# Attention with two branches on one core: the keys' maximum rounded in one step, and three orders given to the planner

## The chip, the cores and the metric

The kernel runs on one core of a Trainium2 chip. The metric is the device time of one execution in microseconds. The program is ordered by hand-written planning code: five engines (TensorE or PE for matmuls, VectorE or DVE, ScalarE or ACT, GpSimd or POOL, and SP, which only issues transfers) each run their own list of instructions, and wait for each other through semaphores.

## What is computed

The input `x` has 2048 rows of 512. Branch A is full attention with 32 heads of 16 dimensions, branch B attends to 8 earlier rows at a distance of 2; the two results are mixed by a gate of each row.

```
g = sigmoid((x * gate_w).sum(-1))
A: q, k, v = x @ A_wqkv;  p = softmax(q k^T / 4) over all 2048 keys;  a = (p v) @ A_wo
B: q, k, v = x @ B_wqkv;  keys and values at s, s-2, ..., s-14;       b = (p v) @ B_wo
out = g * a + (1 - g) * b
```

## The kernel before

**Branch A.** The 2048 queries are cut into 4 chunks of 512 columns, the 32 heads into 8 groups of 4. A pair of (chunk, group) is a *period*: 32 of them, in this order. In a period each of the 4 heads meets 16 tiles of 128 keys; one such meeting is a *unit*: a score matmul of 128 keys x 512 queries, an exponential, and a matmul of the result with the values. Most units go to ScalarE, in *sets* of 3 and 2 units that alternate between two score buffers in PSUM (`rA`, `rB`, the tile `ring`): TensorE writes `ring` from `kt_all` (keys) and `qt` (queries), ScalarE writes `pT` by one ACTIVATE of 1536 or 1024 columns, TensorE multiplies `pT` with `vp_all` (values with a column of ones, for the denominator) into an accumulator. In every period some units (3 at first, 12 from the ninth on) go to VectorE instead, which approximates the exponential by integer arithmetic: `dt_a` or `wkv` from the scores, then three shifted copies `pd_a`, multiplied with scaled values `vd_all`.

Instead of the row's maximum, the scores get a bound: a query's 32 rows of `qt` hold it and its absolute values, the keys' rows hold the keys and, in the other half, minus the largest absolute key (`negk`). `k_proj` projects one group's keys for one chunk of rows, and its VectorE instruction also leaves the maximum over 512 columns in `kmax_all`. `k_bound` (L663) then takes the maximum of four such columns (`mx`), swaps rows with two matmuls against `perm` (`sw`, which wants 16-bit operands: `kmax_b`), makes `negk` of it (`ng`), and writes it into the keys (`fill`). For the first group this stands on the way to the first exponential.

**Other producers.** `v_proj` projects values; for the first group of heads it is called twice, for tiles 0 to 7 and 8 to 15, with 32 matmuls each. `q_proj` projects the queries of the first two periods; `q_pair` those of two later periods at once, which go through DRAM (`q_scr`) and come back by two transfers on SP. Branch B (`b_tile`) projects its keys and values (`bw`), sends them through DRAM (`kv_scr`, `ksh`, `vsh`) and works mostly on POOL.

**The order.** Every step is an `Op` with an engine, an expected length, a due time (`dl`), dependencies, buffers that it takes, and an earliest time (`rel`). `list_schedule` goes through them once as the program is built, with its own clock, takes on each engine the step that is due first among those that can start, and may put filler matmuls on zeros (`z`) between TensorE's steps so that it stays busy. Three PSUM banks (tile `misc_ps`) serve all projections, VectorE's scores and the accumulator. The result is one fixed list for each engine. So a changed due time, length or earliest time can change the lists everywhere behind it. `S0[p]` is the planned start of period p.

Of the kernel before, what the change touches and what calls it, by code (L numbers as in the profile page):

```python
# [9 lines left out]
ALU = mybir.AluOpType  # L10
AX = mybir.AxisListType
FP32 = mybir.dt.float32
# [16 lines left out]
NG = 8  # L29
# [73 lines left out]
QD = 20.0  # L103
# [198 lines left out]
def kernel(  # L302
# [26 lines left out]
    const = ctx.enter_context(tc.tile_pool(name="const", bufs=1))  # L329
# [37 lines left out]
    V = Chained(nc.vector, "dve")  # L367
# [22 lines left out]
    def op(eng, occ, fn, dl, **kw):  # L390
        if any(tk.kind == "misc" for tk in kw.get("use", ())):
            dl -= URG[eng]
        o = Op(eng, occ, fn, dl, **kw)
        ops.append(o)
        return o
# [61 lines left out]
    S0 = [T0 + UNIT * f for f in first_unit]  # L457
# [25 lines left out]
    vp_all = const.tile([128, NT, H, DH + 1], BF16, name="vp_all")  # L483
    vd_all = const.tile([128, NV - 1, NTD, H, DH + 1], BF16, name="vd_all")
    kmax_all = const.tile([128, NG, NC], FP32, name="kmax_all")
    kmax = const.tile([128, NG], FP32, name="kmax")
    kmax_b = const.tile([128, NG], BF16, name="kmax_b")
    negk = const.tile([128, NG], FP32, name="negk")
    dt_a = const.tile([128, NDE * NGR * QW], BF16, name="dt_a")
# [153 lines left out]
    o_kc = {}  # L643
# [20 lines left out]
    def k_bound(i, dl):  # L664
        st = {}
        tk = tok("acc", 1) if i == 0 else tok("misc", 2)

        def mx():
            V.tensor_reduce(out=kmax[:, i:i + 1], in_=kmax_all[:, i, :], axis=AX.X, op=ALU.max)
            V.tensor_copy(out=kmax_b[:, i:i + 1], in_=kmax[:, i:i + 1])  # L670

        def sw():
            st["p"] = misc_ps([128, 2], tag="acc" if i == 0 else "misc")
            for e in range(2):
                mm(st["p"][:, e:e + 1], perm[:, e].rearrange("p a b d -> p (a b d)"), kmax_b[:, i:i + 1], True, True)

        def ng():
            V.scalar_tensor_tensor(out=negk[:, i:i + 1], in0=st["p"][:, 0:1], scalar=st["p"][:, 1:2], in1=rowc[:, 2:3],
                                   op0=ALU.max, op1=ALU.mult)

        def fill(s0, s1):
            def s():
                V.tensor_scalar(out=kt_all[:, i, s0:s1], in0=kt_all[:, i, s0:s1], scalar1=rowc[:, 1:2],
                                scalar2=negk[:, i:i + 1], op0=ALU.mult, op1=ALU.add)
            return s
        a = op("dve", 0.4, mx, dl - 2.5, deps=o_kc[i])
        b = op("pe", 0.1, sw, dl - 2.0, full=0, deps=[a, o_perm], alloc=[tk])
        c = op("dve", 0.2, ng, dl - 1.2, deps=[b], use=[tk])
        if i == 0:
            o_k[i] = [op("dve", 0.0, fill(sc * QW, (sc + 1) * QW), dl + 0.1 * sc, deps=[c], parts=SB(QW)) for sc in range(NC)]  # L690
        else:
            o_k[i] = [op("dve", 0.0, fill(0, S), dl, deps=[c], parts=SB(S))] * NC
# [14 lines left out]
    def v_proj(h0, h1, tb, TB, tag, dl, rel=0.0):  # L707
        n = (h1 - h0) * DH
        st = {}
        tk = tok(tag, 2 if tag == "misc" else 1)  # L710

        def mk(half):
            def s():
                if half == 0:
                    st["pv"] = misc_ps([128, TB, n], tag=tag)
                for tt in range(half * TB // 2, (half + 1) * TB // 2):
                    t = tb + tt
                    for c in range(DC):
                        mm(st["pv"][:, tt, :], xT[:, c, t * 128:(t + 1) * 128],
                           wkv[:, c, D + h0 * DH:D + h1 * DH], c == 0, c == DC - 1)  # L720
            return s

        def ev():
            V.tensor_copy(out=vp_all[:, tb:tb + TB, h0:h1, 0:DH], in_=st["pv"][:].rearrange("p t (h d) -> p t h d", d=DH))

        t0 = max(tb, NT - NTD)
        nt = tb + TB - t0

        def evd():
            w = wts[:]  # L730
            k0, n_ = t0 - (NT - NTD), (h1 - h0) * (DH + 1)
            V.tensor_tensor(out=vd_all[:, :, k0:k0 + nt, h0:h1, :].rearrange("p m t h d -> p m t (h d)"),
                            in0=_ap(vp_all[:, t0, h0, 0:1], [list(vp_all[:].ap[0]), [0, NV - 1], [H * (DH + 1), nt], [1, n_]]),
                            in1=_ap(w, [list(w.ap[0]), [1, NV - 1], [0, nt], [0, n_]]), op=ALU.mult)
        xs = [o for sc in range(NC) if sc * TPC < tb + TB and (sc + 1) * TPC > tb for o in o_xt[sc]]
        a = op("pe", 0.62, mk(0), dl - 2.0, full=2, deps=[o_wv] + xs, alloc=[tk], rel=rel, name=f"vp{h0}.{tb}")
        b = op("pe", 0.62, mk(1), dl - 1.4, full=2, deps=[a], use=[tk])
        c = op("dve", 0.61, ev, dl, deps=[b, o_init_p], use=[tk])
        for h in range(h0, h1):
            for t in range(tb, tb + TB):  # L740
                o_v[(h, t)] = c
        if nt > 0:
            d = op("dve", 0.0, evd, dl + 2.0, deps=[c], parts=TT((NV - 1) * nt * (h1 - h0) * (DH + 1)))
            for t in range(t0, tb + TB):
                for h in range(h0, h1):
                    o_vd[(h, t)] = d

    v_proj(0, 4, 0, 8, "misc", 6.0)
    v_proj(0, 4, 8, 8, "misc", 7.0)
    for h0, h1, pn in ((4, 8, 1), (8, 16, 2), (16, 24, 4), (24, 32, 6)):  # L750
        TB = 512 // ((h1 - h0) * DH)
        for tb in range(0, NT, TB):
# [6 lines left out]
    def q_proj(pi, tag, dl, rel=0.0):  # L759
        c_, i = periods[pi]  # L760
        st = {}
        tk = tok(tag, 2 if tag == "misc" else 1)
        tq = tok("qt", 4)
        q_tok[pi] = tq

        def part(c0, c1):
            def s():
                if c0 == 0:
                    st["p1"] = misc_ps([128, QW], tag=tag)
                    qt_tiles[pi] = work.tile([128, QW], BF16, name="qt", tag="qt", bufs=4)  # L770
                for c in range(c0, c1):
                    mm_q(st["p1"], c, i, xT[:, c, c_ * QW:(c_ + 1) * QW], c == 0, c == DC - 1)
            return s

        def ev():
            V.tensor_copy(out=qt_tiles[pi][:], in_=st["p1"][:])

        def ab():
            u = qt_tiles[pi][:].bitcast(U32)
            V.tensor_scalar(out=u, in0=u, scalar1=qmask[:, 0:1], scalar2=None, op0=ALU.bitwise_and)  # L780
        a = op("pe", WAVE(2), part(0, 2), dl - 2.6, mode="c", js=list(range(4)) * 2, full=2, deps=[o_q2[i], o_init_d] + o_xt[c_] + ([] if pi else [o_kc[0][1]]), alloc=[tk, tq], rel=rel, after=[last_q[0]], name=f"qp{pi}")
        last_q[0] = a
        b = op("pe", WAVE(2), part(2, DC), dl - 2.0, mode="c", js=list(range(4)) * 2, full=2, deps=[a], use=[tk])
        c = op("dve", 0.61, ev, dl - 0.5, deps=[b], use=[tk, tq])
        o_q[pi] = op("dve", 0.0, ab, dl, deps=[c], use=[tq], parts=SB(QW))

    q_proj(0, "acc", 2.5)
    q_proj(1, "misc", S0[1] - 10.0, rel=Q1REL)

    def q_pair(pi, dl, rel):  # L790
# [41 lines left out]
            o_q[pi + e] = op("sp", 0.5, get(e), dl - 1.0 + e, deps=w, alloc=[q_tok[pi + e]], lat=2.2)  # L832

    for pi in range(2, NP, 2):
        q_pair(pi, S0[pi] - QD, S0[pi - 2] - 2.0)


    st_g = {}
# [28 lines left out]
    a = None  # L867
    for sc in range(NC):
        a = op("pe", 0.9, zmm(sc), GT + sc, full=1, deps=[o_bw, a] + o_xt[sc], alloc=[tzp] if sc == 0 else [],
               use=[tzp] if sc else [], rel=20.0)  # L870
    a = op("act", 0.25, zsig, GT + 5, deps=[a], use=[tzp])
    o_g = op("dve", 0.8, zgate, GT + 6, deps=[a])
    a = op("pe", 1.2, zrows, GT + 8, full=1, deps=[o_g, o_init_p], alloc=[tzr])
# [427 lines left out]
    for k, us in enumerate(sets):  # L1301
# [14 lines left out]
        def ex(st=st, n=n, k=k):  # L1316
# [4 lines left out]
        a = op("pe", 0.0, qk, tn - 3.0, mode="r", js=[u_[2] for u_ in us], deps=[o_q[pi] for pi in pis] + kd,  # L1321
               alloc=[tr_], use=[q_tok[pi] for pi in pis], after=[last_qk[0]], scores=k % 2, name=f"qk{k}")
# [15 lines left out]
    for pi, (c_, i) in enumerate(periods):  # L1338
# [33 lines left out]
        a = op("dve", 0.64, po1, E - PO1D, deps=o_pv[pi], alloc=[ta], use=[acc_tok[pi], acc_two[pi]])  # L1372
        tr_ = tok("rden", 2)
        a = op("dve", 0.29, po2, E + 4.0, deps=[a], alloc=[tr_], use=[ta])
        al, us = [to] if i % 2 == 0 else [], [ta, tr_] + ([to] if i % 2 else [])
        if by_v:
            a = op("dve", 0.0, po2a, E + 4.0, deps=[a, o_gr], use=[tr_], parts=TT(BPC))
            a = op("dve", 0.0, po2b, E + 4.0, deps=[a], alloc=al, use=us, parts=TT(BPC * DH))
        else:
            a = op("pool", 0.0, po2a, GFIRST, deps=[a, o_gr], use=[tr_], parts=GP("ff", BPC))  # L1380
            a = op("pool", 0.0, po2b, GFIRST, deps=[a], alloc=al, use=us, parts=GP("ff", BPC * DH))
# [12 lines left out]
    for t in range(NT):  # L1394
# [6 lines left out]
        dl = E + (4.0 + 4.0 * tt if last else 2.0 + 4.0 * tt)  # L1401
        pin = last and tt < 2
        if pin:
            dl = S0[NP] - 1.0
# [24 lines left out]
        a = None  # L1429
        for k0 in range(0, DC + nh, 2):  # L1430
            nk = min(2, DC + nh - k0)
            a = op("pe", WAVE(nk), ab_part(k0), dl - 2.0 + 0.3 * k0, full=nk,
                   deps=[a] if k0 else [o_oat[NG * c_ + ng - 1], o_wo] + ([d_last[0]] + o_pv[NP - 1][:len(o_pv[NP - 1]) - (8, 0)[tt]] if pin else []) + o_obt[t:t + 1],
# [85 lines left out]
```

## Time and profile before

| | us |
|---|---|
| three runs | 813.45, 817.77, 819.55 (median 817.77) |
| the profiled execution | 813.94 |
| its span, first to last instruction | 812.1 |
| ScalarE busy | 786.6 |
| TensorE / VectorE / POOL busy | 750.9 / 683.8 / 632.6 |
| first exponential starts | 19.61 |

A row of the timeline reads: start in us, duration in us, engine, line, operation, output<-inputs, shape, count of merged instructions, and in brackets the idle time of the engine ahead of it and what ended it. A merged row lasts from its first start to its last end, with other rows of other engines beside it. Nearly all instructions carry line 364 or 373, the helpers through which they are issued, so the tiles tell them apart. Granted clock 0.999 of full speed in this execution.

### The profile page before, as it was taken

What the parts mean: (1) busy time and instruction counts of PE and PEld (TensorE: products, weight loads), DVE (VectorE), ACT (ScalarE), POOL (GpSimd) and SP (SyncE); (2) the same over time, 40 slices, a digit from 0 to 9 for tenths busy, and PEclk for the clock granted to TensorE, in tenths of its full rate; (3) what the DMA queues carried; (4) which work ended last, traced back from release to release, by engine and by line L of the source; (5) the groups of instructions that cost most, each with busy time, mean ns of one, the idle gap of its engine ahead of it and who ended that gap; (6) DMA issues with size and microseconds to landing.
All of it is one profiled execution on the core that took longest, in us unless ns stands there. A gap on an engine that the chain in (4) does not pass through costs nothing.

```text
span 812.1 us, 18026 instructions
## 1 busy us (share of the span) xinstructions
PE 750.9 (92%) x6970; PEld 245.7 (30%) x7025; DVE 683.8 (84%) x1076; ACT 786.6 (97%) x708; POOL 632.6 (78%) x1058
## 2 busy tenths in 40 slices
PE   8999999999999998999889999989989999898997
PEld 4333334324222222222222222323222222222322
DVE  5636776796887999989989899897988899898896
ACT  2999999999999999999999999999999999999996
POOL 3098969889899999999997795979669419899910
PEclk9999999999999999999999999999999999999999
DMA  8403071533545354454525406162440521522000
GB/s 262 136 9 118 2 168 55 136 86 95 140 111 118 92 118 132 103 135 92 144 55 125 122 21 167 43 162 54 90 112 26 125 92 44 153 59 72 1 2 27
DMA packets 58886, 77.22 MB, mean 95 GB/s; under 512 B 3744, under 2 KB 50848, under 8 KB 58800
## 3 DMA queue, kind: packets, MB, share of 16 engines
q1 hardware_dynamic: 52608, 53.91, 21.6%
q0 software_dynamic: 6048, 22.02, 14.5%
q8 instruction: 55, 0.90, 0.5%
q14 instruction: 31, 0.25, 0.1%
q10 hardware_dynamic: 144, 0.13, 0.0%
HBM read 43.78 MB, written 10.26 MB: 67 GB/s over the span
## 4 chain that ended last, share of the span: by engine, by line
ACT 49%; PE 28%; issue 19%; DVE 2%; DMA 1%; SPq 0%; ACTq 0%
ACT pT L364 49%; PE misc_ps L373 19%; PE ring L373 8%; DMA xld<-in_A_x_dram 1%; ACT lg L364 1%; DVE kt_all L364 0%; PE pxt L622 0%; DVE wkv L364 0%; DVE dt_a L364 0%; DVE pd_a L364 0%; DVE accT L364 0%; DVE kvs L364 0%; ACT xT L364 0%; SPq L364 0%; DVE qt L364 0%
## 5 line engine op out<-in xcount | busy, mean ns | idle before, releaser
L364 ACT ACTIVATE pT<-ring 128x1536 bf16<-128x1536 f32 (+1 forms) x684 | 778.6, 1322 | 9.3 <-PE ring L373 8.5
L373 PE MATMUL ring<-qt,kt_all 32*128 32x512 bf16 x1709 | 269.7, 382 | 46.8 <-ACT pT L364 37.7
L364 POOL TENSOR_TENSOR prod<-ksh,qb 128x256 f32<-128x256 bf16 x256 | 174.7, 739 | 60.4 <-DMA ksh<-kv_scr 58.6
L373 PE MATMUL misc_ps<-pT,vp_all 128*17 128x512 bf16 (+1 forms) x1709 | 208.6, 383 | 0.1
L373 PEld LDWEIGHTS <-kt_all 32*128 32x128 bf16 x2048 | 88.9, 91 | 301.2 <-issue 291.8
L364 DVE TENSOR_SCALAR pd_a<-wkv 128x1536 uint16<-128x1536 uint16 x192 | 175.5, 942 | 1.6 <-PE misc_ps L373 0.6
L364 POOL TENSOR_TENSOR prod<-prod 128x256 f32<-128x256 f32 (+1 forms) x256 | 166.7, 665 | 5.8
L364 DVE TENSOR_SCALAR wkv<-misc_ps 128x512 uint16<-128x512 f32 x192 | 129.2, 684 | 27.7 <-PE misc_ps L373 23.2
L373 PE MATMUL misc_ps<-z 128*32 128x512 bf16 x428 | 141.3, 386 | 1.6 <-DVE z L364 1.6
L364 DVE TENSOR_SCALAR pd_a<-dt_a 128x1536 uint16<-128x1536 uint16 x147 | 135.5, 944 | 1.0
L373 PE MATMUL misc_ps<-pd_a,vd_all 128*17 128x512 bf16 x1017 | 132.0, 381 | 0.1
L373 PE MATMUL misc_ps<-qt,kt_all 32*128 32x512 bf16 x339 | 124.9, 380 | 2.5 <-DVE accT L364 0.6
L364 DVE TENSOR_SCALAR dt_a<-misc_ps 128x512 uint16<-128x512 f32 x147 | 99.2, 685 | 18.7 <-PE misc_ps L373 16.9
L364 POOL TENSOR_TENSOR prod<-vsh,lg 128x256 f32<-128x256 bf16 x128 | 81.5, 734 | 0.0
L364 POOL TENSOR_TENSOR av<-vsh,lg 128x256 f32<-128x256 bf16 x128 | 79.7, 656 | 0.0
L373 PEld LDWEIGHTS <-vp_all 128*17 128x17 bf16 (+1 forms) x2048 | 54.5, 88 | 79.9 <-issue 66.2
L373 PEld LDWEIGHTS <-z 128*32 128x32 bf16 x428 | 37.7, 96 | 50.7 <-issue 28.1
L373 PE MATMUL misc_ps<-bw,xT 128*128 128x512 bf16 x164 | 50.6, 383 | 2.5 <-issue 1.1
L373 PEld LDWEIGHTS <-vd_all 128*17 128x17 bf16 x1017 | 35.0, 88 | 46.9 <-issue 37.6
L364 POOL DMA_DIRECT2D av<-av x14 | 12.3, 879 | 38.1 <-DMA av<-prod 37.8
L373 PEld LDWEIGHTS <-xT 128*128 128x128 bf16 x576 | 29.5, 97 | 33.0 <-issue 28.7
L373 PE MATMUL misc_ps<-xT,wkv 128*32 128x512 bf16 x384 | 37.9, 382 | 0.0
(90 smaller groups left out, 577.5 us busy)
## 6 DMA issues: line engine op xcount, KB each, us to landing
ksh<-kv_scr SPq DMA_DIRECT2D x32, 512.0 KB
vsh<-kv_scr SPq DMA_DIRECT2D x32, 512.0 KB
av<-prod POOLq DMA_DIRECT2D x28, 512.0 KB, 5.8
av<-av POOLq DMA_DIRECT2D x14, 512.0 KB, 5.1
kv_scr<-kvs SPq DMA_DIRECT2D x16, 256.0 KB
qt<-q_scr SPq DMA_DIRECT2D x30, 128.0 KB
q_scr<-qs SPq DMA_DIRECT2D x15, 128.0 KB
q_scr<-qa SPq DMA_DIRECT2D x15, 128.0 KB
```

The lines of the kernel that those rows point to most:

```text
L364: return chain_on(key, f(*a, **k))
L373: return chain(nc.tensor.matmul(out, lhsT=lhsT, rhs=rhs, start=start, stop=stop, **kw))
```

## The change

Four edits. In `k_bound` the reduction writes its result straight to the 16-bit tile `kmax_b`; the 32-bit tile `kmax` and the cast between them go, and the step's expected length falls from 0.4 to 0.2. The two value projections of the first heads get an earliest time of 18.6. The first queries' due time goes from 2.5 to 0.0. The queries of the pairs of periods get an earliest time of at least 19.0, which binds for the first pair alone (third and fourth period), whose earliest time was 15.0.

```diff
-    kmax = const.tile([128, NG], FP32, name="kmax")
...
         def mx():
-            V.tensor_reduce(out=kmax[:, i:i + 1], in_=kmax_all[:, i, :], axis=AX.X, op=ALU.max)
-            V.tensor_copy(out=kmax_b[:, i:i + 1], in_=kmax[:, i:i + 1])
+            V.tensor_reduce(out=kmax_b[:, i:i + 1], in_=kmax_all[:, i, :], axis=AX.X, op=ALU.max)
...
-        a = op("dve", 0.4, mx, dl - 2.5, deps=o_kc[i])
+        a = op("dve", 0.2, mx, dl - 2.5, deps=o_kc[i])
...
-    v_proj(0, 4, 0, 8, "misc", 6.0)
-    v_proj(0, 4, 8, 8, "misc", 7.0)
+    v_proj(0, 4, 0, 8, "misc", 6.0, rel=18.6)
+    v_proj(0, 4, 8, 8, "misc", 7.0, rel=18.6)
...
-    q_proj(0, "acc", 2.5)
+    q_proj(0, "acc", 0.0)
...
-        q_pair(pi, S0[pi] - QD, S0[pi - 2] - 2.0)
+        q_pair(pi, S0[pi] - QD, max(19.0, S0[pi - 2] - 2.0))
```

## The prediction

> **What bounds the kernel now.** I read the page from the top: first the busy shares, then the slices, then the chain that ended last, and after it the groups of ScalarE alone.
>
> ```profile
> span 812.1 us, 18026 instructions
> PE 750.9 (92%) x6970; PEld 245.7 (30%) x7025; DVE 683.8 (84%) x1076; ACT 786.6 (97%) x708; POOL 632.6 (78%) x1058
> ...
> ACT  2999999999999999999999999999999999999996
> ...
> PEclk9999999999999999999999999999999999999999
> ...
> ACT 49%; PE 28%; issue 19%; DVE 2%; DMA 1%; SPq 0%; ACTq 0%
> ```
>
> ScalarE (ACT) is busy for 786.6 of 812.1 us; only its first and last slices are not full. The chain changes between ACT and PE all the time, because two score buffers are handed to and fro: TensorE fills one while ScalarE takes the exponential of the other. So the time is ScalarE's work, plus what passes before its first exponential, plus its gaps, plus the tail. Two more views, ScalarE's groups and its waits, size the second and the third:
>
> ```profile
> L364 ACT ACTIVATE pT<-ring 128x1536 bf16<-128x1536 f32 x342 | 524.0, 1532 | 9.3 <-PE ring L373 8.5 <-PE misc_ps L373 0.2
> L364 ACT ACTIVATE pT<-ring 128x1024 bf16<-128x1024 f32 x341 | 379.7, 1114 | 0.0
> ...
> ACT pT L364 <- PE ring L373: 8.5, 8, 5.1
> ```
>
> Of 9.3 us that ScalarE idled ahead of exponentials, 5.1 is the one wait for the first of them and 4.2 is all the rest of the run. The changed kernel issues the same 684 exponentials, so nothing in 786.6 us is removed. What can move is the start, the 4.2 us of gaps, and the tail. A gain of 1% (8 us, about what a measurement of this kernel can tell from no change) isn't there to be had: all gaps and the whole wait of 5.1 us make 9.3.
>
> **The start, step by step.** The timeline from 16.55 us to the first exponential:
>
> ```profile
> 16.55 1.11 PE L373 MATMUL misc_ps<-wkv,xT 128*128 128x64 bf16 x32
> 16.61 0.16 DVE L364 TENSOR_REDUCE kmax<-kmax_all 128x1 f32<-128x4 f32 x1
> 16.80 0.16 DVE L364 CAST kmax_b<-kmax 128x1 bf16<-128x1 f32 x1
> 16.87 0.68 DVE L364 CAST qt<-misc_ps 128x512 bf16<-128x512 f32 x1
> ...
> 17.50 0.19 PE L373 MATMUL misc_ps<-kmax_b,perm 128*128 128x1 bf16 x2
> ...
> 17.58 0.35 DVE L364 TENSOR_SCALAR qt<-qt,qmask 128x256 uint32<-128x256 uint32 x1
> 17.60 1.09 PE L373 MATMUL misc_ps<-wkv,xT 128*128 128x64 bf16 x32
> 17.85 0.69 DVE L364 CAST vp_all<-misc_ps 128x512 bf16<-128x512 f32 x1
> 18.45 0.21 DVE L364 SCALAR_TENSOR_TENSOR negk<-misc_ps,rowc 128x1 f32<-128x1 f32 x1
> 18.70 0.74 DVE L364 TENSOR_SCALAR kt_all<-kt_all,rowc,negk 128x512 bf16<-128x512 bf16 x2
> ...
> 19.17 0.60 PE L373 MATMUL ring<-qt,kt_all 32*128 32x512 bf16 x5 [0.48 <-DVE kt_all L364]
> ...
> 19.61 1.45 ACT L364 ACTIVATE pT<-ring 128x1536 bf16<-128x1536 f32 x1 [5.09 <-PE ring L373]
> ```
>
> VectorE (DVE) is the path: maximum, its rounding, the queries' cast and mask, a cast of values, negk, the fill of the keys; then scores, then the exponential. The order of the changed kernel's instructions there is
>
> ```
> VectorE: kmax_b reduce, qt cast, qt mask, negk, kt_all fill x4, vp_all cast x2
> TensorE: first queries (16), perm (2), z (1), values (32), scores (5), values (32),
>          pair queries (2), scores (3), pair queries (2), scores (2), ...
> ```
>
> (a) *The maximum written as 16 bits* removes one cast of 0.16 us. It costs the path less: the queries' cast started at 16.87, only 0.07 after it. Gain 0.07; bounds 0 and 0.19 (the next operation waits for nothing of the maximum and could follow 0.07 after 16.61, as it followed the cast, so at 16.68 instead of 16.87). I take 0.07. The Trainium skill, "VectorE: DVE Perf Modes", section "The DRAIN you can't avoid", says that the next operation does not start until the pipe is empty, and adds that one which isn't held starts earlier. By the first sentence the cast would be worth its 0.16; the trace agrees with the second. The same edit in the seven later head groups saves 7 x 0.16 = 1.1 us on an engine with 128 us to spare: nothing, hidden under ScalarE; without that cover 1.1 us.
>
> (b) *First values held back.* Their cast at 17.85 stood 0.60 us ahead of negk (18.45), and it leaves. Negk then follows the mask, if the two perm matmuls are done: without the 32 value matmuls in front they start about 16.9 instead of 17.50, so they are. Gain 0.60. What is late next is TensorE: perm, a filler and 32 value matmuls stand before the first scores. From 16.9 at 0.10 for perm (17.50 to 17.60), some 0.2 for the filler and 1.09 for the values this ends near 18.3; the scores become ready at 19.17 - 0.67 = 18.50. Cover 0.2 us. If the value matmuls must wait for the query cast's bank (about 17.5), they end at 18.6, and the gain shrinks to 0.57.
>
> (c) *First queries with deadline 0*: the 16 query matmuls stand at the same place on TensorE in both orders, and the cast behind the maximum in both. Nothing, bounds 0 and 0.1.
>
> (d) *Third period's queries held back.* Four matmuls move behind the second 32 values; between first and second triple of scores TensorE has 32 values (1.09) and two query matmuls. The rows after the start:
>
> ```profile
> 19.71 1.04 PE L373 MATMUL misc_ps<-xT,wq 128*128 128x512 bf16 x3
> ...
> 21.14 0.39 PE L373 MATMUL ring<-qt,kt_all 32*128 32x512 bf16 x3
> ```
>
> and the busy times by stage (stretch, its length, then PE, PEld, DVE, ACT, POOL, clock, DMA share, GB/s), with SP's queue after them:
>
> ```profile
> 20.00:25.00 5.00, 4.66 (x58) 2.12 (x61) 4.35 (x9) 5.00 (x5) 0.00 (x0) 1.00 0.14 35
> ...
> 26.20 0.83 SPq L364 DMA_DIRECT2D qt<-q_scr  x2
> 27.08 0.42 SPq L364 DMA_DIRECT2D bwo<-in_B_wo_dram  x1
> 27.55 4.73 SPq L364 DMA_DIRECT2D woarr<-in_A_wo_dram  x8
> ...
> 36.57 0.94 SPq L364 DMA_DIRECT2D ksh<-kv_scr  x2
> ```
>
> Before, queries and 16 values lay there, and from 20 to 25 us ScalarE was busy 5.00 of 5.00 (fourth engine of the row). After: scores at 18.50, next work 0.54 later as before (19.17 to 19.71), 1.09 + 0.43: the third set's scores go at 20.6 instead of 21.14. The second exponential's end, 0.67 earlier too, waits for them no more than it did. Cost 0, bounds 0 and 0.3. On SP's queue one of the two loads of `qt` (26.20) falls behind bwo, the eight woarr loads and the first ksh pair, to about 37 us. It belongs to the fourth period, which starts past 100 us; POOL waits for ksh anyway and is not the bound. Cost 0; without the 60 us of slack it would be the 11 us of the delay.
>
> Start: 0.07 + 0.60 = **0.67 earlier**, bounds 0.5 and 0.9.
>
> **The gaps in the middle.** All work behind is ordered anew by the planner. ScalarE's timeline, rows with a wait:
>
> ```profile
> 42.68 3.77 ACT L364 ACTIVATE pT<-ring 128x1536 bf16<-128x1536 f32 x3 [0.23 <-PE ring L373]
> 82.72 27.57 ACT L364 ACTIVATE pT<-ring 128x1536 bf16<-128x1536 f32 x24 [0.86 <-PE ring L373]
> 113.29 22.89 ACT L364 ACTIVATE pT<-ring 128x1536 bf16<-128x1536 f32 x20 [0.43 <-PE ring L373]
> 137.04 19.94 ACT L364 ACTIVATE pT<-ring 128x1536 bf16<-128x1536 f32 x17 [0.87 <-PE ring L373]
> 172.14 28.66 ACT L364 ACTIVATE pT<-ring 128x1536 bf16<-128x1536 f32 x25 [0.39 <-PE ring L373]
> 208.97 35.50 ACT L364 ACTIVATE pT<-ring 128x1536 bf16<-128x1536 f32 x31 [0.17 <-PE ring L373]
> 277.93 4.62 ACT L364 ACTIVATE pT<-ring 128x1536 bf16<-128x1536 f32 x4 [0.43 <-PE ring L373]
> ```
>
> and TensorE's ahead of the second of these:
>
> ```profile
> 81.12 0.40 PE L373 MATMUL misc_ps<-xT,wkv 128*32 128x512 bf16 x3
> ...
> 81.33 0.40 PE L373 MATMUL misc_ps<-xT,wkv 128*32 128x512 bf16 x3
> ...
> 82.23 0.60 PE L373 MATMUL ring<-qt,kt_all 32*128 32x512 bf16 x5
> ```
>
> Seven gaps, 3.4 us. Nearly every one follows the same picture: a long burst of projections and value products on TensorE, and then five score matmuls in one run (82.23), the triple so late that it meets the pair behind it. Such runs can be counted in the two orders: past the first, 17 before and 14 after. The bursts can be weighed too, 0.21 us for a group of four strips (81.12 to 81.33). The burst ahead of 82.23 weighs 1.6 and cost 0.86; it is there unchanged. Ahead of 137.04 stood 1.7; that one is gone, but three new ones weigh 1.9, 2.3 and 2.0 (at the key projections of later groups; by their places among the 1709 score matmuls, which run from 19.6 to about 804 us (the tail, below), near 56, 105 and 132 us: an estimate).
>
> At the most that a burst has cost so far, three make 2.6; with the unchanged 0.86 and some 0.4 of small ones (of 1.2 before, as the runs of five are fewer) 3.9 us: **0.5 more than now**. By the number of runs alone it would be 14/17 of 3.4, 0.6 less; by weight, see below, 2.7 more. I stay near the lower end, because heavy bursts of before (weights 1.2 to 1.5) often cost nothing. From the middle on the two orders agree for long stretches.
>
> **The tail.** ScalarE's last exponentials:
>
> ```profile
> 779.24 24.79 ACT L364 ACTIVATE pT<-ring 128x1536 bf16<-128x1536 f32 x22
> ```
>
> They end at 804.0, 8.1 before the end of the span. The last 195 matmuls and the last 40 VectorE rows stand in the same order in both kernels: 0.
>
> Sum: -0.7 + 0.5 = **-0.2 us**. The profiled execution took 813.94 (span 812.1, 1.84 around it) and would take 813.7. It is one of the quicker ones: the three runs are 813.45, 817.77 and 819.55. Since an execution of either kernel may fall anywhere there, I set the sum on the mean of the four, 816.2, not on the median of 817.77: **816.0**.
>
> **Rivals.** *Forecast*, the start gained and the middle a little worse: 816.0, chance 0.50.
>
> *The new bursts starve ScalarE* (the other side: slower). Place: the three bursts named. Price: if a gap grows one to one with weight beyond 1.6, they cost 1.2, 1.55 and 1.3, with 0.86 and the 1.2 of small ones 6.1 us against 3.4: +2.7, and with the start +2.0: 818.2. It decides once a burst outlasts what the two exponentials in hand cover. For it: same kind of burst, 0.86 and 0.87. Against: weight alone did not decide before. 0.30.
>
> *The new order lands better*: two gaps fewer of the large kind, 1.6 us in all: -0.7 - 1.8, 813.7. For it: fewer runs of five. 0.13.
>
> *The change doesn't reach the start*: the 32 values on TensorE hold back the first scores until 19.1. Then only the middle counts: 816.7. Against: the 0.2 us of cover worked out in (b). 0.04.
>
> *TensorE loses its clock*: three fillers (z) fewer, and a bare wait for the maximum near 16.7. At half rate the 4.66 us of TensorE work in 20 to 25 us would take 9.3, and ScalarE would lose 4.3: 820.3. Against: the clock row is 9 throughout and the wait is some 0.3 us. 0.03. The Trainium skill, "TensorE: Matmul & The Clock Gate", section "What's actually happening", lets the clock fall only after an idle window of about 3.4 us; the trace of before has no such stretch to show it.
>
> **How the numbers follow.** The cases reach from 813.7 to 818.2 without the last; a median of a few executions out of a spread of 6 us adds some 2 on either side: 812.0 to 820.5. None of the cases is 1% away from 817.77 (809.6, 825.9); only unseen stalls or a lucky or poor set of executions lead there: faster 0.03, within 0.94, slower 0.03.
>
> **What would show it.** First exponential at 18.9 (18.7 to 19.1) instead of 19.61, negk straight after the mask, no kmax cast. ScalarE's idle ahead of exponentials 8.2 to 9.7 instead of 9.3, its busy time within 1 us of 786.6, and the distance from the last exponential to the end as now. Gaps above 1 us near 56, 105 and 132 us would show the second case; a clock row below 9 the last. The forecast is wrong if a wait for a DMA or for VectorE appears ahead of scores, or ScalarE's exponentials themselves change in length.

## The result, and the profile after

| | before | after |
|---|---|---|
| median of 22 executions each, us | 816.73 | 814.85 |
| lowest and highest | 813.45, 820.7 | 814.62, 817.45 |
| the profiled execution (its span) | 813.94 (812.1) | 816.37 (814.6) |

The ratio on record is 0.9976 with an interval of 0.9964 to 0.9987: 1.9 us or 0.24% less, within the 1% that was called no change. But the two profiles say the opposite: the profiled execution of after is 2.4 us *longer*. Both are true, and the way from the one to the other is what the experiments are about. A profile is one draw; before's was a quick one, after's a long one.

The page of after, busy shares and the chain that ended last:

```profile
span 814.6 us, 18016 instructions
PE 754.1 (93%) x6969; PEld 247.2 (30%) x7022; DVE 685.0 (84%) x1068; ACT 786.8 (97%) x708; POOL 633.1 (78%) x1058
...
ACT 49%; PE 24%; issue 21%; DVE 3%; DMA 2%; SPq 1%; ACTq 0%; DVEq 0%
```

ScalarE does the same 786.8 us of work. Its groups (count, busy, mean ns, idle ahead and what ended it) and, in the fence behind, its waits (total, times, longest):

```profile
L364 ACT ACTIVATE pT<-ring 128x1536 bf16<-128x1536 f32 x342 | 526.5, 1539 | 11.9 <-PE ring L373 9.3 <-PE misc_ps L373 2.0
L364 ACT ACTIVATE pT<-ring 128x1024 bf16<-128x1024 f32 x341 | 381.8, 1120 | 0.1
```

```profile
ACT pT L364 <- PE ring L373: 9.3, 7, 4.4
ACT pT L364 <- PE misc_ps L373: 2.0, 3, 1.4
```

Idle time rose from 9.3 to 11.9 although the wait for the first exponential fell from 5.1 to 4.4. So 7.5 us lie in the rest of the run, where before had 4.2. The start first, from after's timeline (start, duration, engine, operation, in brackets the idle time ahead):

```profile
16.21 0.16 DVE L364 TENSOR_REDUCE kmax_b<-kmax_all 128x1 bf16<-128x4 f32 x1
16.28 0.69 DVE L364 CAST qt<-misc_ps 128x512 bf16<-128x512 f32 x1
16.51 0.19 PE L373 MATMUL misc_ps<-kmax_b,perm 128*128 128x1 bf16 x2 [0.29 <-DVE kmax_b L364]
17.00 0.35 DVE L364 TENSOR_SCALAR qt<-qt,qmask 128x256 uint32<-128x256 uint32 x1
17.08 1.09 PE L373 MATMUL misc_ps<-wkv,xT 128*128 128x64 bf16 x32
17.27 0.22 DVE L364 SCALAR_TENSOR_TENSOR negk<-misc_ps,rowc 128x1 f32<-128x1 f32 x1
...
18.10 0.60 PE L373 MATMUL ring<-qt,kt_all 32*128 32x512 bf16 x5
18.54 3.71 ACT L364 ACTIVATE pT<-ring 128x1536 bf16<-128x1536 f32 x3 [4.42 <-PE ring L373]
```

From the reduction to the first exponential it takes 18.54 - 16.21 = 2.33 us; before it was 19.61 - 16.61 = 3.00. That is the 0.67. The other 0.40 between 19.61 and 18.54 is not the change's: the whole execution was ahead by that much at the reduction already (16.21 against 16.61; the second profile of before, below, has it at 16.30).

Then ScalarE's rows that had a wait ahead of them:

```profile
54.54 13.75 ACT L364 ACTIVATE pT<-ring 128x1536 bf16<-128x1536 f32 x12 [1.45 <-PE misc_ps L373]
68.55 8.23 ACT L364 ACTIVATE pT<-ring 128x1536 bf16<-128x1536 f32 x7 [0.26 <-PE ring L373]
83.37 22.71 ACT L364 ACTIVATE pT<-ring 128x1536 bf16<-128x1536 f32 x20 [0.86 <-PE ring L373]
107.27 2.37 ACT L364 ACTIVATE pT<-ring 128x1536 bf16<-128x1536 f32 x2 [1.19 <-PE ring L373]
112.56 23.03 ACT L364 ACTIVATE pT<-ring 128x1536 bf16<-128x1536 f32 x20 [0.29 <-PE misc_ps L373]
136.59 20.45 ACT L364 ACTIVATE pT<-ring 128x1536 bf16<-128x1536 f32 x18 [1.00 <-PE ring L373]
167.97 33.45 ACT L364 ACTIVATE pT<-ring 128x1536 bf16<-128x1536 f32 x29 [1.38 <-PE ring L373]
212.10 31.79 ACT L364 ACTIVATE pT<-ring 128x1536 bf16<-128x1536 f32 x28 [0.21 <-PE ring L373]
775.06 31.50 ACT L364 ACTIVATE pT<-ring 128x1536 bf16<-128x1536 f32 x28 [0.23 <-PE misc_ps L373]
810.36 1.07 ACT L364 CAST osb<-misc_ps 128x512 bf16<-128x512 f32 x2 [3.79 <-PE misc_ps L373]
```

The three bursts named beforehand (near 56, 105 and 132 us) are there, at 54.5, 107.3 and 136.6: 1.45, 1.19 and 1.00 us. The old one is unchanged at 0.86. The gap of 1.38 at 167.97 is of another kind. The busy times by stretches of 4 us (stretch, length, then PE, PEld, DVE, ACT, POOL, granted clock, DMA share, GB/s) show it:

```profile
160.00:164.00 4.00, 2.83 (x26) 0.99 (x23) 3.74 (x7) 4.00 (x4) 3.79 (x7) 1.00 0.47 89
164.00:168.00 4.00, 4.00 (x24) 0.67 (x22) 3.12 (x7) 2.51 (x4) 3.64 (x6) 0.57 0.56 111
```

From 160 to 164 TensorE was busy for 2.83 of 4.00 us only. In the next stretch its granted clock was 0.57, it was busy all the time and did no more than 24 matmuls, and ScalarE starved. Such a stretch is called a *dip* below. In before's profile every such stretch but the last shows 1.00.

### The profile page after: what moved, and what is told of

It is laid out like the page before. It is cut to its first block, busy times and chain, and to the rows that moved or that the text cites. A ratio compares the mean times of both kernels' runs of the same rounds, so it can differ in the third digit from the quotient of the medians.

```text
span 814.6 us, 18016 instructions
## 1 busy us (share of the span) xinstructions
PE 754.1 (93%) x6969; PEld 247.2 (30%) x7022; DVE 685.0 (84%) x1068; ACT 786.8 (97%) x708; POOL 633.1 (78%) x1058
## 4 chain that ended last, share of the span: by engine, by line
ACT 49%; PE 24%; issue 21%; DVE 3%; DMA 2%; SPq 1%; ACTq 0%; DVEq 0%
ACT pT L364 48%; PE misc_ps L373 16%; PE ring L373 8%; DMA xld<-in_A_x_dram 1%; ACT lg L364 1%; SPq L364 1%; DMA woarr<-in_A_wo_dram 0%; DVE pd_a L364 0%; DMA q_scr<-qa 0%; DVE accT L364 0%; PE pxt L621 0%; DVE qs L364 0%; DVE qa L364 0%; DVE kt_all L364 0%; DVE kvs L364 0%
## 5 line engine op out<-in xcount | busy, mean ns | idle before, releaser
L373 PE MATMUL misc_ps<-pT,vp_all 128*17 128x512 bf16 (+1 forms) x1709 | 205.6, 384 | 1.7 <-DVE accT L364 1.1
L373 PE MATMUL misc_ps<-z 128*32 128x512 bf16 x425 | 138.2, 387 | 1.6 <-DVE z L364 1.6
L364 POOL TENSOR_TENSOR prod<-vsh,lg 128x256 f32<-128x256 bf16 x128 | 84.2, 758 | 0.0
L373 PE MATMUL misc_ps<-xT,wk 128*32 128x512 bf16 x128 | 35.8, 381 | 0.0
```

The source lines that it names most:

```text
L364: return chain_on(key, f(*a, **k))
L373: return chain(nc.tensor.matmul(out, lhsT=lhsT, rhs=rhs, start=start, stop=stop, **kw))
```

## The experiments

All ratios are to executions of before on the same chip, taken together with the kernel's own. Times are medians in us, with the lowest, the highest and the number of executions. A ratio is worked out from all executions of both sets, so it can differ from the quotient of the two medians.

**The two kernels once more.** Unchanged, to see how much two sets of executions differ, and whether time follows clock.

> The kernel before, once more, so that the granted clock of each of its executions is seen. Theory 'clock' (the spread of the kernel before, 813.5 to 820.7 us, comes from short stretches in which TensorE's clock is lowered, and its new order has fewer of them): executions near 813.5 have a mean clock of 0.999 or 1.000, each that is slower by 1.3 to 1.5 us has about 0.003 less, and most executions have at least one such stretch. Theory 'noise' (the spread is in transfers or elsewhere): the clock is 0.999 in all, whatever the time.

> The changed kernel, once more, for a profile that may have no stretch of lowered clock. Theory 'clock': without one its span is 813.0, its exponentials' idle time is near 10.4 us (11.9 less the 1.4 at 168 us), 1.1 more than in the kernel before, and its executions stay within 0.4 us of each other except for those with a lower mean clock. Theory 'noise': the gap at 168 us is there in every execution.

Before again: 816.24 (813.63 to 817.69, 12 executions), ratio 0.9998 [0.998, 1.0015]. After again: 814.99 (814.72 to 817.64, 12), ratio 0.9994 [0.9978, 1.0011] to a before that came out at 816.28 (35 executions). So the advantage of after is small against the spread of before: the ratio was 0.9976 the first time and 0.9994 the second, where the interval includes 1 (the medians alone have 0.9977 and 0.9984). What differs clearly is the spread. By mean granted clock over the execution:

| clock | before, 47 executions | after, 34 executions |
|---|---|---|
| 0.999 and 1.0 | 15: 813.42 to 815.86 | 27: 814.62 to 815.00 |
| 0.998, 0.997 | 19: 814.85 to 817.39 | 4: 816.02 to 816.37 |
| 0.996 and less | 13: 817.07 to 820.99 | 3: 817.45 to 817.64 |

After has the longer quick execution (814.8 against 813.5) and far fewer long ones. Its dips also wander: in this second profile none stands at 168 us, but ScalarE waits 0.98 at 362.19 and 1.22 at 409.20, where the clock rows read 0.76 to 0.81 and 0.74 to 0.84. And there is a second source: six of before's executions ran at full clock and still took 814.8 to 815.9. The third digit of the clock tells them apart. Over all executions of before that were taken for the experiments, 14 of the 16 executions at 0.999 took 813.4 to 814.1, and 14 of the 15 at 1.000 took 814.8 to 816.0. In before's profile (0.999) the lost thousandth is a dip that starts at 810.96, behind the last exponential, where it costs nothing. Neither profile of before is of the longer kind (813.94 and 813.69), so what makes those executions longer was not seen in before itself.

**The maximum alone, on unchanged lists.**

```diff
-            V.tensor_reduce(out=kmax[:, i:i + 1], in_=kmax_all[:, i, :], axis=AX.X, op=ALU.max)
-            V.tensor_copy(out=kmax_b[:, i:i + 1], in_=kmax[:, i:i + 1])
+            V.tensor_reduce(out=kmax_b[:, i:i + 1], in_=kmax_all[:, i, :], axis=AX.X, op=ALU.max)
```

The planned length stays 0.4, so every engine's list is the one of before without eight casts.

> Only the eight casts go; the planned length of the step stays at 0.4, so all orders are those of the kernel before. Prediction's term (a): first exponential 0.07 us sooner, the time within 0.1 us of the kernel before. Rival: the seven later casts were on the path too, 0.5 to 1.2 us less.

816.23 (813.27 to 820.14, 12), ratio 0.9999 [0.9977, 1.0022]; its profiled execution took 813.29. ScalarE's first wait is 5.01 us against 5.09 in the second run of before: 0.08, where 0.07 had been worked out.

**The maximum with its planned length of 0.2.** The same edit, and `op("dve", 0.2, mx, ...)`.

> Only the 16-bit maximum, with its planned length of 0.2. The planner then orders all anew (about a fifth of TensorE's list stays in place). Theory 'the start is one term, the order another': first exponential 0.07 us sooner, and gaps that have nothing to do with the edit, between 3 and 9 us; the median anywhere between 813.5 and 819. Rival 'the 16-bit maximum is the gain': 1 to 2 us quicker in the median.

814.67 (812.97 to 816.8, 10), ratio 0.9969 [0.995, 0.9989]. The first wait is again 5.01 us. So the cast is worth 0.08, and what else came is due to one planned length that is 0.2 us shorter: the planner ordered everything anew. Its four executions at a clock of 0.999 or more took 812.97 to 815.19, among them the shortest of all kernels that compute everything. Its median is not to be told from after's.

**The values alone.** Of the four edits only `rel=18.6`.

> Only the first values' earliest time of 18.6. Theory 'start': first exponential 0.60 us sooner after the reduction than before, gaps between 3 and 9 us by the new order, the median anywhere between 813.5 and 819. Rival 'holding the values back is the whole gain': the median of the changed kernel, 814.9, with its narrow spread.

819.61 (817.84 to 825.12, 10), ratio 1.0038 [1.0015, 1.0062]. The expectation failed: the start came later, not earlier. VectorE's timeline of this kernel:

```profile
17.41 0.21 DVE L364 SCALAR_TENSOR_TENSOR negk<-misc_ps,rowc 128x1 f32<-128x1 f32 x1
17.72 0.69 DVE L364 CAST qs<-misc_ps 128x512 bf16<-128x512 f32 x1
18.33 1.05 DVE L364 TENSOR_SCALAR kt_all<-kt_all,rowc,negk 128x512 bf16<-128x512 bf16 x3
19.29 0.69 DVE L364 CAST vp_all<-misc_ps 128x512 bf16<-128x512 f32 x1
...
20.21 0.35 DVE L364 TENSOR_SCALAR qt<-qt,qmask 128x256 uint32<-128x256 uint32 x1
```

The hole that the values left was filled by the third period's queries (`qs`), and the mask of the first queries, due at 2.5 and so behind the fills, came last of all. ScalarE's first wait grew to 6.59 us.

**All but the first queries' deadline.**

```diff
-    q_proj(0, "acc", 0.0)
+    q_proj(0, "acc", 2.5)
```

> All of the change but the deadline of the first queries, which stays at 2.5. The lists are those of the changed kernel but for fillers and one place: VectorE masks the first queries behind the four fills of the keys instead of ahead of negk. Theory 'the mask gates the first scores': they wait for it, behind four fills that start about 0.1 us apart from the changed kernel's and end 1.3 later; first exponential 0.9 to 1.4 us later than in the changed kernel, counted from the reduction (2.33 there), so the deadline is worth about 1 us together with the held values though alone it changes no list. Prediction's term (c): nothing, at most 0.1 us.

815.58 (815.37 to 816.9, 10), ratio 0.9989 [0.9975, 1.0002]. Its start, from the timeline of all engines:

```profile
16.22 0.16 DVE L364 TENSOR_REDUCE kmax_b<-kmax_all 128x1 bf16<-128x4 f32 x1
...
17.14 1.38 DVE L364 TENSOR_SCALAR kt_all<-kt_all,rowc,negk 128x512 bf16<-128x512 bf16 x4
...
18.43 0.35 DVE L364 TENSOR_SCALAR qt<-qt,qmask 128x256 uint32<-128x256 uint32 x1
...
18.84 0.59 PE L373 MATMUL ring<-qt,kt_all 32*128 32x512 bf16 x5 [1.17 <-DVE qt L364]
...
19.27 1.45 ACT L364 ACTIVATE pT<-ring 128x1536 bf16<-128x1536 f32 x1 [5.14 <-PE ring L373]
```

The mask stands behind the four fills here, and the scores wait 1.17 us for it. From reduction to exponential 3.05 us: 0.72 more than after, and the median is 0.7 above after's. Its later gaps are after's (1.47, 0.86, 1.19 and 1.00 us). Alone, this deadline changes no list at all, and neither do the held-back queries alone; together with the values they decide.

**The start alone.** The list of before, with only the steps up to 23 us put by hand into after's order, and without the casts.

```diff
+    put_after(named("kb_sw0")[0], named("vp0.0") + named("bv0.0"))
+    put_after(named("qk1")[0], named("vp0.8") + named("bv0.8") + named("qp2")[:1])
...
+    put_after(named("kb_f3")[0], named("vc0.0") + named("vc0.8"))
```

> The order of the kernel before is kept from about 23 us on; only the 16-bit maximum and the place of the first values (behind negk and the fills, as in the changed kernel) are taken from the change. Theory 'start and order are separate': the first exponential comes 0.67 us sooner after the reduction than before (2.33 us instead of 3.00), the gaps stay as before (4.2 us), the quickest executions are 0.7 us under the quickest of the kernel before, near 812.8, and the spread stays, so that the median is 0.7 lower. Rival 'the start sets all': the median falls to that of the changed kernel or below, by 1.9 us, with its narrow spread.

817.33 (813.3 to 820.71, 12), ratio 1.0007 [0.9983, 1.003]. The first wait fell to 4.31 us, so the start is gained by itself; but 0.33 and 0.29 us came back at 23.7 and 26.3, and before's spread stayed. Its profile, with no dip ahead of its last exponential, shows what the second source can be. ScalarE lost 1.01 us at 582.02. TensorE had waited 1.05 us for a cast on VectorE (`kvs`), and the cast for one operation ahead of it (`qa`); GpSimd's row of the same time stands in a fence of its own:

```profile
578.65 1.69 DVE L364 TENSOR_SCALAR qa<-qs 128x256 uint32<-128x256 uint32 x1
580.26 0.68 DVE L364 CAST kvs<-misc_ps 128x512 bf16<-128x512 f32 x1
580.99 0.59 PE L373 MATMUL misc_ps<-bw,xT 128*128 128x512 bf16 x2 [1.05 <-DVE kvs L364]
```

```profile
577.49 2.69 POOL L364 TENSOR_TENSOR prod<-vsh,lg 128x256 f32<-128x256 bf16 x4
```

`qa` took 1.69 us, and ended (580.34) just behind GpSimd's run of four multiplications (577.49 + 2.69 = 580.18). In the second run of before the same operation came just ahead of that run, and took 0.48 (VectorE's row, then GpSimd's):

```profile
578.63 0.48 DVE L364 TENSOR_SCALAR qa<-qs 128x256 uint32<-128x256 uint32 x1
```

```profile
578.89 2.77 POOL L364 TENSOR_TENSOR prod<-vsh,lg 128x256 f32<-128x256 bf16 x4
```

`qa` makes the absolute queries of later periods, and the casts behind it on VectorE free the PSUM banks that TensorE waits for. Its length over the 15 instances (minimum, median, maximum in ns), of before and then of start_only:

```profile
L364 DVE TENSOR_SCALAR qa<-qs x15: 283/294/714, 22.2 to 730.0; 128x256 uint32<-128x256 uint32 x15
```

```profile
L364 DVE TENSOR_SCALAR qa<-qs x15: 283/466/1692, 22.4 to 731.0; 128x256 uint32<-128x256 uint32 x15
```

**No hold by another operand.** If `qa` is held because both its ends lie in SBUF, it shouldn't be when it reads PSUM. In the list of before, `qa` takes the upper halves of the 32-bit queries straight from PSUM (cut off instead of rounded, so the bound moves a little). It also moves: it becomes part of the step of the cast `qs` and stands directly behind it, where before had it up to 24 us later.

```diff
+            pu = st["p"][:].bitcast(U16)
+            V.tensor_scalar(out=st["a"][:].bitcast(U16), in0=_ap(pu[:, 1:2], [list(pu.ap[0]), [2, QW]]), scalar1=0x7FFF, scalar2=None,
```

> The kernel before, with one change: the absolute queries (qa, 15 operations of VectorE) are made from the upper halves of the projection in PSUM, not from the SBUF copy (so they are cut instead of rounded, which moves the bound and not the result). Theory 'two sources' (beside the clock, a qa operation that meets a run of POOL instructions is held until that run ends, as in the profile where it took 1.69 us instead of 0.29): all 15 last 0.6 to 0.7 us, and the executions with a clock of 0.999 or 1.000, which in the kernel before lie at 813.4 to 815.9, stay within 0.5 us of each other. The clock's part of the spread stays. Rival: qa is not the source; the executions at full clock spread over 2 us as before.

`qa` now takes 0.675 to 0.682 us every time, though GpSimd was at work beside 14 of the 15. 817.69 (816.09 to 819.28, 12), ratio 1.0007 [0.9991, 1.0022]. The four executions at full clock lie at 816.09 to 816.35, within 0.26 us instead of 2.4. So `qa` is no longer held, at a price: the operation is 0.4 us longer and the quickest execution 2.4 us (before's on the same chip took 813.69). That the second source is gone is not shown by this: the four lie above even the longer executions that before had at a clock of 1.000 on this chip (815.8 to 816.0), so all of them may be long for another reason, such as the new place of `qa` or the PSUM bank that it now holds for longer. The dips stayed (down to 0.995, 819.28).

**GpSimd's work cut short.** The other side of the same pair: the list of before with GpSimd's long operations on 16 instead of 256 columns past the first tile, a constant read for the sums `lg`, and accumulating transfers of 32 columns. The local attention's values aren't computed.

```diff
+                n = HB if t == 0 else 16
+                G.tensor_tensor(out=st["prod", hf, wp][:, w_, c0:c0 + n], in0=st["ksh", hf][:, wp + w_, c0:c0 + n],
+                                in1=st["qb"][:, c0:c0 + n], op=ALU.mult)
```

> The kernel before, with GpSimd's long multiplications and additions cut short: the products prod, av and the halving sums work on 16 columns instead of 256 past the first tile, the sums lg read a constant, and the accumulating transfers carry 32 columns; so the local attention's values are not computed. The order of every engine's instructions stays that of the kernel before. Theory (the mask operation qa and the key fills of VectorE are held until a run of GpSimd's operations ends): with no long run left, qa takes 0.28 to 0.35 us every time instead of 0.28 to 0.8 and the 2048-wide fills 0.81 to 0.9; the executions at a mean clock of 0.999 or more lie within 0.4 us of each other, near 813.5, instead of 813.4 to 815.9; those below 0.999 stay longer, up to 818, and the median falls by 0.5 to 1.5 us. Rival (the hold comes from something else, as transfers or VectorE's own queue): qa still reaches 0.6 us and more, and executions at full clock still spread over 2 us.

814.46 (813.32 to 814.67, 12), ratio 0.9971 [0.9952, 0.999], beside a before of 813.44 to 820.72. GpSimd's busy time falls from 632.6 to 308.5 us, and `qa` to its bare length, but for one instance beside a long operation of the first tile:

```profile
L364 DVE TENSOR_SCALAR qa<-qs x15: 280/283/609, 22.0 to 730.8; 128x256 uint32<-128x256 uint32 x15
```

Five executions at a clock of 0.999 took 813.32 to 813.50. The other seven took 814.39 to 814.67: one step of 1.1 us higher, and nothing beyond. The profiled one (814.63) is of the second kind and shows what the step is (busy times by stretch, then ScalarE's timeline):

```profile
136.00:140.00 4.00, 3.02 (x25) 1.02 (x24) 3.92 (x9) 3.20 (x3) 0.15 (x1) 1.00 0.00 0
140.00:144.00 4.00, 3.64 (x33) 1.37 (x32) 3.01 (x4) 3.79 (x4) 2.49 (x12) 0.57 0.02 4
```

```profile
144.96 12.93 ACT L364 ACTIVATE pT<-ring 128x1536 bf16<-128x1536 f32 x11 [1.15 <-PE ring L373]
```

A single dip, after a stretch in which TensorE was busy for 3.02 of 4.00 us, costs ScalarE 1.15 us, and the execution is longer by that much. (The other six were not profiled.) The list of before has the same thin stretch (3.03 of 4.00 in its own profile) without a dip behind it, and the profile of qa_psum, which has before's order but for `qa`, has the dip there again (granted clock 0.68 from 140 to 144 us): the place is the list's, whether the clock drops there differs from execution to execution. The expectation had the executions below 0.999 go on to 818. That was wrong, in favour of the theory: without long operations on GpSimd the executions at 0.996 and less, 13 of 47 with before and 5 of the 17 taken beside this kernel, don't occur in 12.

**The fillers.** After with both kinds of fillers cut to 8 columns (they compute nothing that is used).

```diff
-                mm(tz[0:32, :], z32[:], z_bc, True, True, tile_position=(0, 0))
+                mm(tz[0:32, 0:8], z32[:], z32[:, 0:8], True, True, tile_position=(0, 0))
```

> The changed kernel with its 425 filler matmuls on zeros cut from 512 columns to 8; they compute nothing that is used, and the order is the same. Theory 'clock': TensorE has more stretches without work, its clock is lowered more often, the mean granted clock falls below 0.99, and each lowered stretch costs 1 to 1.5 us: slower by 5 us or more, with a spread at least that of the kernel before. Rival 'the fillers only cost': TensorE has 425 x 0.2 us less to do, ScalarE's gaps get shorter, the time falls by 1 to 4 us.

828.92 (827.42 to 831.2, 4), ratio 1.0147 [1.0115, 1.0179], mean clock 0.945 to 0.955. So matmuls on zeros are worth 14 us here, and less load on TensorE does bring dips: its profile has 14 ahead of the last exponential, where after's two profiles have one and two.

What comes ahead of a dip is best read in steps that fit its edges. In every profile a dip ahead of the last exponential has the clock at 0.50 for 3.41 us, or for two or three times that, and dips of one execution begin a whole number of such steps apart (164.25 and 812.78 in after: 190 steps). The step ahead of a dip and the dip's first step, in after, after_no_fill and v_only (its longest of 10.24 us in after_no_fill):

```profile
160.84:164.25 3.41, 2.24 (x22) 0.90 (x19) 3.38 (x8) 3.30 (x5) 3.04 (x6) 1.00 0.61 115
164.25:167.66 3.41, 3.41 (x17) 0.45 (x15) 2.53 (x4) 2.34 (x2) 3.30 (x6) 0.50 0.60 120
```

```profile
599.14:602.55 3.41, 2.17 (x25) 0.78 (x24) 2.65 (x4) 3.41 (x4) 2.87 (x5) 1.00 1.10 296
602.55:605.96 3.41, 3.39 (x23) 0.77 (x22) 1.51 (x4) 3.41 (x4) 3.25 (x7) 0.50 0.37 83
```

```profile
277.89:281.30 3.41, 3.08 (x20) 0.75 (x18) 3.37 (x7) 3.41 (x5) 3.11 (x6) 1.00 0.98 198
281.30:284.71 3.41, 3.41 (x20) 0.85 (x17) 3.21 (x7) 2.61 (x4) 2.69 (x6) 0.50 0.91 245
```

Counted so over all 14 profiles (past the first 20 us and up to 12 us before the end, steps at full clock alone), 17 of the 29 steps in which TensorE was busy for less than 2.3 us have a dip behind them, 7 of the 280 with 2.3 to 2.8 us, and 1 of the 2853 with more (the last pair above). So a thin step makes a dip likely and not certain.

The Trainium skill, "TensorE: Matmul & The Clock Gate", section "What's actually happening", has the clock halve after an idle window of about 3.4 us, in windows that run freely and so fall differently in each execution. The rows agree with the half (0.50 over a whole step), with the length of the step and with the varying place, but none of these three dips follows an idle window: TensorE was busy for 2.24, 2.17 and 3.08 of the 3.41 us ahead.

**Two attempts at a better kernel.** k_start is k_only's list with after's start put in by hand; k_start_qa writes `qa` in addition as 16-bit data in two rows of 256.

> The order of the single edit k_only behind 25 us, and the changed kernel's place of the first values at the start. Theory 'separate terms': 2.33 us from the reduction to the first exponential instead of 2.93, gaps after it as in k_only (3.9 us), quickest executions near 812.4, under both kernels; the spread of k_only (4 us) stays, the median is near 814. Rival: the start's gain is given back in the first ten sets, as in start_only (0.62 us there), and the median is that of k_only, 814.7.

> k_start, with the absolute queries made by 16-bit operands read as two rows of 256 and written as one of 512 (the shape by which the shifted copies pd_a, 339 operations, always lasted 0.89 to 0.96 us). Theory 'held by POOL only in the two-word form': all 15 qa last within 0.1 us of each other, executions at full clock spread by 0.5 us instead of 2, and the median falls below k_start's by 0.3 to 1 us. Rival: the form is held as the other is (a maximum over 1 us), and nothing changes.

k_start: 815.61 (813.49 to 817.5, 12), ratio 0.9985 [0.9969, 1.0]. From reduction to exponential 2.23 us, so the start is won once more, but a wait of 0.85 us at 26.35 gives it back. k_start_qa: 815.66 (813.2 to 818.7, 12), ratio 0.9983 [0.9967, 0.9999]; `qa` took 0.28 to 2.52 us, so this form is held too. No version is clearly better than after in the median.

## Why the prediction was right, and where it was not

The time, 814.85, lies in the range and 1.2 us under the 816.0. Several terms were off and nearly cancelled; the steps:

- **(a) The cast, 0.07: right.** 0.08 measured on unchanged lists. What a shorter planned length does to the rest of the lists was left to the count of bursts, and is worth more than the cast (k_only).
- **(b) The values, 0.60, and (c) the deadline, nothing: right as a sum, wrong as terms.** The whole start is 2.33 us instead of 3.00, the 0.67 of the forecast, and negk, fills and scores stand as listed. (That it fits to the hundredth is luck: start_only and k_start, with the same order at the start, took 2.23.) But (c) was priced by the place of the query matmuls in both lists, and what it moves is the mask: without it, 0.72 is lost (no_d). And (b) alone makes the start worse (v_only, 6.59 us). The three are one term; bounds of 0 and 0.1 for (c) held only for the deadline put into before by itself.
- **(d) The third period's queries, 0:** there was no stall between the first sets of scores in after, whose first wait past the start stands at 54.5 us. Its list is needed for (b), as v_only shows.
- **The gaps, +0.5: the mis-sized term.** In an undisturbed execution they grow from 4.2 to about 6.1 us (7.5 less the 1.38 of the dip): +1.9. The three bursts were found at their places, but taken at 0.87 at most each (2.6 together); they cost 1.45, 1.19 and 1.00, and the small ones of the rows up to 300 us 0.76 where 0.4 was expected. The second case's rule, one to one with weight beyond 1.6, had 1.2, 1.55 and 1.3: nearer in the sum (4.05 against 3.64), though the heaviest was not the dearest. The argument against it, that lighter bursts of before often cost nothing, said nothing on heavier ones. Its 1.2 us of small gaps was misread: those of its seven rows that are neither 0.86 nor 0.87 sum to 1.65, so that case would have had +3.2 and not +2.7.
- **The tail, 0, and ScalarE's busy time:** right (3.79 us ahead of the last cast, 786.8).
- **The sum, -0.2:** for undisturbed executions it is -0.67 + 1.9 = +1.2, and the measured floors give 814.8 - 813.5 = +1.3. By its sign, gaps of 1 us and more at the three places, the second case came true there, though its +2.7 for the gaps was too much; ScalarE's idle time, 10.5 us without the dip, also lies above the 8.2 to 9.7 that the forecast had named.
- **The basis, 816.2: the step that was wrong.** The spread of the four executions of before was taken as noise that either kernel would have. It belongs to the list: before's median of 816.73 lies 3.2 us above its own quick executions, after's 814.85 lies at them. +1.3 - 3.2 = -1.9, which is the measured difference. A clock dip was in the forecast only as one event of 4.3 us at the start, with a chance of 0.03; it comes as events of 1.0 to 1.4 us, anywhere, and by the mean clock in two thirds of before's executions (32 of 47 below 0.999). So the forecast was 0.5 too low in its basis (816.2 for a median of 816.73) and 1.5 too low in its sum (-0.2 for +1.3), and 3.2 too high for the spread that it carried over to after. That these leave only 1.2 us is luck.

What stays open is why the list of after meets fewer dips. `qa` is held there just as long (up to 1.42 and 1.48 us in its two profiles), and one hold of 1.17 us stands just ahead of the dip of after's profile:

```profile
161.55 1.17 DVE L364 TENSOR_SCALAR qa<-qs 128x256 uint32<-128x256 uint32 x1
162.63 0.70 DVE L364 STREAM_TRANSPOSE accT<-misc_ps 128x512 f32<-128x512 f32 x1
163.39 0.40 PE L373 MATMUL misc_ps<-pT,vp_all 128*32 128x512 bf16 x4 [1.10 <-DVE accT L364]
```

TensorE waited 1.10 us for the transpose behind the held `qa`; the clock fell at 164.25, and ScalarE lost 1.38. In the second profile of after the same hold (1.07 us at 161.62) and the same wait (1.00 us) stand at this place, without a dip and without a wait of ScalarE. So a held `qa` can cost twice: by the wait itself, as in start_only, and by a step thin enough for a dip. That this is the usual way to a dip is argued from these two places, not shown. Thin steps alone don't explain the count either: under 2.4 us, after's two profiles have four steps each and before's two none and one. Both profiles of before are of quick executions without a dip ahead of 810 us, so the dips of its longer ones weren't seen one by one. That GpSimd's long work, its transfers included, makes before's spread is shown by pool_short; that it does so through `qa` and the fills alone isn't, since shorter operations also hand their own results over sooner.

## What to carry to other kernels

Ahead of any argument in tenths of a microsecond, sort the executions of a kernel by their granted clock: the floor and the spread are two results, an edit can move them in opposite directions, and a profile shows one draw of both. Where a planner makes the order, an edit's price includes what moves into the hole that it leaves; one edit on unchanged lists, and the edit with its re-planning, are two experiments. A stretch of 3.4 us in which TensorE is busy for only two thirds is worth filling, even with matmuls on zeros.

## What the runs showed of the hardware

- TensorE's granted clock fell to 0.50 for 3.41 us or two or three times that, at places a whole number of such steps apart, in some executions and not in others of the same list. Of the steps in which TensorE was busy for less than 2.3 us, 17 of 29 had such a dip behind them; of those with 2.3 to 2.8 us, 7 of 280; of all others, 1 of 2853. One dip cost 1.0 to 1.4 us of ScalarE's time in the profiles of after and pool_short; without full-width fillers the mean clock was 0.95 and the kernel 14 us longer.
- A VectorE operation from SBUF to SBUF (`qa`, 0.28 us alone) took longer beside GpSimd's operations. Often the wait ended with the one operation of GpSimd that was under way: in before, `qa` took 0.71 us from 160.30, beside one from 160.23 to 160.86. In some places it lasted over two or three operations of a run: up to 2.17 us in k_start, and 2.52 in the 16-bit form of k_start_qa. The 2048-wide fill of the keys took 0.81 alone (0.809 mean in pool_short) and up to 3.28 in k_only. `pd_a`, also from SBUF to SBUF, took 0.89 to 0.96 us in all its 339 instances, beside GpSimd's runs or not. The Trainium skill, "SBUF — State Buffer", section "SBUF: two separate sides", describes a port pair that GpSimd and some VectorE operations lock for a whole instruction, so that the other waits in full. The shorter waits agree with that; the long ones lasted more than one instruction: in start_only GpSimd's four took 2.69 us together, 0.67 each, and `qa` was held for 1.69 - 0.28 = 1.4, until the run ended. What makes the one kind or the other isn't known.
- Made from PSUM, in a 16-bit form and at another place in the list, `qa` was never held (0.675 to 0.682 us, 15 of 15).
